# Down products paired across batch groups, products reordered and the down weights loaded later, in a fused attention and gated feed-forward kernel

## The chip, the cores and the metric

The kernel runs on one core of a Trainium2 chip. The metric is the time of one execution on the device, in microseconds (us); three runs of the kernel before gave 400.8, 400.87 and 401.26, and the median, 400.87, is its time.

The core has engines that work side by side, each through its own list of instructions in order: TensorE (PE: matrix products; PEld: the loading of their stationary operand), VectorE (DVE), ScalarE (ACT), GpSimd (POOL) and SyncE (SP). They wait for each other by semaphores. DMAs are issued from the lists of SP, ACT and POOL. A product's result lies in one of eight PSUM banks and must be read out by VectorE or ScalarE before the bank is used again.

## The reference

```python
# batch 8, 12 heads, 448 tokens, head_dim 64; d_model 768, d_ff 1536
scores = scale * np.matmul(q, k.transpose(0, 1, 3, 2)) - np.log(S)
attn = 1.0 / (1.0 + np.exp(-scores))
attn_out = np.matmul(attn, v)
x = attn_out.transpose(0, 2, 1, 3).reshape(B * S, H * D)      # 3584 x 768
gate = np.maximum(x @ w_gate, 0.0)
val = x @ w_val
out = gate * val @ w_out                                      # 3584 x 768, float32
```

## The kernel before

**Attention.** Batches 0 to 7 follow each other. A batch has three groups of four heads, and each group seven units of 64 keys: 21 qk units in all. A qk unit is four small products on quarters of the array into two banks, and two sigmoids on ScalarE into a PT tile. When a group's seven units are done, `pv_group` multiplies with v (28 small products, "pv"), and VectorE copies the two results into xT (`put_xT`, L184). The keys and queries are transposed by DMA from batch 2 on: VectorE copies them into `rel` (two copies for each group, L215) and SP issues the transpose into `qkT` (`dma_transposes`). `hold` is a copy of two elements on POOL that waits until such a transpose has landed, so that POOL's next load is issued behind it.

**Feed-forward.** Batches 0 and 1 form group 0, then 2 and 3 group 1, and so on. For group 0, gate and value are computed directly: `gv` makes one of 12 column blocks for one batch (two runs of six products of 448 columns) and VectorE writes relu(gate) * value into hT (L327). For groups 1 to 3 a "w" unit (`gv_pair`) does two column blocks for two batches with seven block products in place of eight (Strassen's scheme in Winograd's form). For the output, a "y" unit (`down_pair`) does two tiles of 128 tokens, tiles 2p and 2p+1, with seven products of six matmuls of 384 columns. With A the hT blocks (A11, A12 of the first tile, A21, A22 of the second; the second index is the half of d_ff) and B the four blocks of wo, the sums are S1 = A21+A22, S2 = S1-A11, S3 = A11-A21, S4 = A12-S2 and T1 = B12-B11, T2 = B22-T1, T3 = B22-B12, T4 = B21-T2, and the products are

P1 = A11 B11, P2 = A12 B21, P3 = S4 B22, P4 = A22 T4, P5 = S1 T1, P6 = S2 T2, P7 = S3 T3.

They are issued as P1 P5 P6 P2 P7 P3 P4, in y and in w units. P1, P6, P7 and P4 add up in one bank (u), P5 and P3 in a second, P2 has a third; in between, ScalarE and VectorE copy the partial sums out. Each group has 896 tokens, which is seven tiles: three y units and one odd tile, "t" (`down`), with twelve matmuls of 512 and twelve of 256 columns.

**Order.** In each batch the 21 qk units are dealt out over five or six stretches m (`cuts`). At the end of each stretch comes either a number of gv (`mix`, with `hooks` between them), or one unit of `work` by `next_work`; such a unit with its stretch is called a slot (a "y slot", a "w slot"). Stretches are counted from 0. `prepare` computes the sums (S) that the unit at the head of `work` needs; in a y unit it is called just before P4, so all four S of the following unit are made there by `token_sums`. `beside` runs the stretch's `jobs` (transposes, loads, sums of the next group's xT: `batch_sums_t1`, `batch_sums`). `gate_sums` turns wv's first half into wg-wv, which groups 1 to 3 need; `weight_sums` makes T1 to T4 of wo. Both are VectorE work.

In the kernel before, the order around the change is: wo is loaded in batch 1's last stretch, on POOL ahead of batch 3's k, q and v; T1 to T4 are made in batch 2's last two stretches; the first y unit (y0 of group 0) closes batch 2; the odd tile of group 0 stands in batch 3's stretch 3, followed by all six gate sums at once; y1 and y2 follow in batch 3's last stretch and batch 4's first. Group 1 starts in batch 4's stretch 1 and takes ten stretches (six w, t, y0, y1, y2), group 2 the next ten, and group 3 follows alone. The last pv stands between y1 and y2 of group 2.

Of the kernel before, what the change touches and what calls it, by code (L numbers as in the profile page):

```python
# [17 lines left out]
def kernel(  # L18
# [143 lines left out]
    def load_o():  # L162
        for m0, m1 in ((0, 512), (512, DM)):
            nc.gpsimd.dma_start(
                wo[:, :, m0:m1], moe_w_out[:, m0:m1].rearrange("(c p) m -> p c m", p=P)
            )
# [96 lines left out]
    class FirstSlot:  # L263
# [6 lines left out]
        def unit(self, u):  # L270
# [8 lines left out]
            i = (self.number * 4 + u) % 12  # L279
            PT = early.tile([P, 2, 512], FP16, tag=f"PT{i}", name="PT")  # L280
# [22 lines left out]

    def gv(b, q0, qn, f, act_relu):
# [19 lines left out]
        if g not in hT_tiles:  # L324
            hT_tiles[g] = hTp.tile([P, NFC, 2 * S], FP16, tag="hT", name="hT")
        o = (b % 2) * S + q0
        nc.vector.tensor_tensor(  # L327
            out=hT_tiles[g][:, f, o : o + qn],
            in0=gate_sb[:, 0:qn],
            in1=ps[1][:, 0:qn],  # L330
            op=AOP.mult,
        )
# [8 lines left out]
    def down(g, t):  # L341
        ysb = ysbp.tile([P, DM], FP32, tag="ysb", name="ysb")
        for nm, m0, m1 in (("ya", 0, 512), ("yb", 512, DM)):
            ps = bank(nm)
            for f in range(NFC):
                nc.tensor.matmul(  # L346
                    ps[:, 0 : m1 - m0],
                    hT_tiles[g][:, f, t * P : (t + 1) * P],
                    wo[:, f, m0:m1],
                    start=(f == 0),  # L350
                    stop=(f == NFC - 1),
                )
            nc.vector.tensor_scalar(
                out=ysb[:, m0:m1], in0=ps[:, 0 : m1 - m0], scalar1=OUT_SCALE, scalar2=None, op0=AOP.mult
            )
        store(g, t, ysb, 0, DM, (nc.sync, nc.sync))

# [7 lines left out]
    late = {}  # L365
    sums = {}

    def open_late():
        first_sbuf.close()
        pool = ctx.enter_context(tc.tile_pool(name="late", bufs=1))  # L370
        late["T"] = pool.tile([P, 4, HF, HM], FP16, tag="T", name="T")
        late["X"] = pool.tile([P, 3, HD, S], FP16, tag="X", name="X")
        late["sums"] = ctx.enter_context(tc.tile_pool(name="sums", bufs=2))
# [20 lines left out]

    def weight_sums(i):
        T = [late["T"][:, j] for j in range(4)]
        B11, B21 = wo[:, 0:HF, 0:HM], wo[:, HF:NFC, 0:HM]
        B12, B22 = wo[:, 0:HF, HM:DM], wo[:, HF:NFC, HM:DM]
        sub(T[i], *((B12, B11), (B22, T[0]), (B22, B12), (B21, T[1]))[i])

    def token_blocks(g, p):
        h = hT_tiles[g]
        t1, t2 = (slice(t * P, (t + 1) * P) for t in (2 * p, 2 * p + 1))
        return h[:, 0:HF, t1], h[:, HF:NFC, t1], h[:, 0:HF, t2], h[:, HF:NFC, t2]

    def token_sums(g, p):
# [3 lines left out]
        sub(S2, S1, A11)  # L410
        sub(S4, A12, S2)
        sub(A21, A11, A21)
        sums[("y", g, p)] = S1, S2, S4
# [9 lines left out]
    def down_pair(g, p, beside, then, last, first_copy):  # L423
        A11, A12, S3, A22 = token_blocks(g, p)
        S1, S2, S4 = sums.pop(("y", g, p))
        T1, T2, T3, T4 = (late["T"][:, i] for i in range(4))
        B11, B21, B22 = wo[:, 0:HF, 0:HM], wo[:, HF:NFC, 0:HM], wo[:, HF:NFC, HM:DM]
        y1, y2 = (ysbp.tile([P, DM], FP32, tag="ysb", name="ysb") for _ in range(2))
        lo, hi = slice(0, HM), slice(HM, DM)
        b, c, a = bank("u"), bank("y12"), bank("y11")  # L430
        later((7, 6, 5))
# [10 lines left out]
        first_copy(y1[:, lo], b)  # L442
        beside()
        product(c, S1, T1)
# [3 lines left out]
        product(a, A12, B21)  # L448
        plus(y1[:, lo], a)
        product(b, S3, T3, False)  # L450
        plus(y2[:, hi], b)
        product(c, S4, B22, False)
        plus(y1[:, hi], c)
        if last:
            store(g, 2 * p, y1, 0, DM, (nc.sync, nc.scalar))
        else:
            store(g, 2 * p, y1, 0, DM, (nc.sync, nc.sync))
# [3 lines left out]
        if last:  # L461
            store(g, 2 * p + 1, y2, HM, DM, (nc.sync, nc.sync))
            store(g, 2 * p + 1, y2, 0, HM, (nc.sync, nc.scalar))
        else:
            store(g, 2 * p + 1, y2, 0, DM, (nc.sync, nc.sync))
# [7 lines left out]
    def unit_sums(g, f):  # L473
        S1, S2, S4 = sums_tile(2 * P)
        fs = slice(f * P, (f + 2) * P)
# [5 lines left out]
        sums[("w", g, f)] = S1, S2, S4  # L481
# [10 lines left out]
    def batch_sums(g, ks):  # L492
        T1, T2, T4, _, B21, B12, B22 = batch_blocks(g, ks)
        sub(B12, B22, B12)
        sub(T2, B22, T1)
        sub(T4, B21, T2)

    def gv_pair(g, f, beside, first_copy):
# [3 lines left out]
        b, c, a = ([bank(nm) for _ in range(2)] for nm in ("u", "g2", "g1"))  # L502
        later((6, 7, 4, 5, 2, 3))
        gs = [[gsbp.tile([P, S], FP32, tag="gsb", name="gsb") for _ in range(3)] for _ in range(2)]
        if g not in hT_tiles:
            hT_tiles[g] = hTp.tile([P, NFC, 2 * S], FP16, tag="hT", name="hT")
        h = hT_tiles[g]
        sets = []
        for u in range(2):
            us, fs = slice(u * P, (u + 1) * P), slice((f + u) * P, (f + u + 1) * P)  # L510
            S1, S2, S4 = (t[:, :, us] for t in sums[("w", g, f)])
            sets.append((
                wg[:, 0:HD, fs], wg[:, HD:NDC, fs], wv[:, HD:NDC, fs],
                S1, S2, wv[:, 0:HD, fs], S4,
# [280 lines left out]
```

## Time and profile before

| what | us |
| --- | --- |
| median of three runs | 400.87 |
| the profiled execution, its own time | 400.93 |
| its span, first to last instruction | 399.2 |
| TensorE busy | 388.9 |
| VectorE busy | 279.9 |
| ScalarE busy | 223.0 |
| GpSimd busy | 49.4 |
| mean granted TensorE clock | 0.999 |

In a timeline each row is a run of equal instructions: start from the span's start, time from the first's start to the last's end, engine, line, operation, result<-inputs, shapes, count, and in brackets the idle time of the engine before it and what ended it. A row of TensorE ends later than the next one begins, as matmuls overlap; the time that a product takes of TensorE is therefore read from start to next start. Rows of "u", "y" and "g" on L385 are block products, "ya" and "yb" the odd tile, "g_ps" and "v_ps" a gv.

### The profile page before, as it was taken

Reading aid. Unit: us, or ns where it says so; the run is one execution under the profiler, and the core shown is the slowest. Engines: PE = TensorE matmul, PEld = TensorE weight load, DVE = VectorE, ACT = ScalarE, POOL = GpSimd, SP = SyncE. Lnnn points to the kernel's source line nnn. Section 1 sums busy time; section 2 is a strip of 40 time slices with the busy share of each in tenths; the row PEclk is TensorE's granted clock in tenths of the full one; section 3 lists DMA queues with packets and bytes.
Section 4 is the critical chain, followed back from the end, with each engine's and each line's share of the span. In section 5 each row is a group of like instructions: output and inputs, shape, how many; then the busy total and the mean of one; then the engine's idle time right before and its main releaser. Section 6 shows DMA issues by size and latency. Waiting matters only on the chain.

```text
span 399.2 us, 8737 instructions
## 1 busy us (share of the span) xinstructions
PE 388.9 (97%) x3488; PEld 217.9 (55%) x3488; DVE 279.9 (70%) x539; ACT 223.0 (56%) x475; POOL 49.4 (12%) x73
## 2 busy tenths in 40 slices
PE   8999999999998999999999999999999999999994
PEld 3678786545455554554555555455455555555562
DVE  2454344367358889999758889999766779887661
ACT  5946778783885565655665455565566234533131
POOL 8643301600030300003000300000000000000000
PEclk9999999999999999999999999999999999999999
DMA  9999994999897894224945695223012320000144
GB/s 149 199 199 204 205 141 94 177 203 187 178 161 152 165 204 76 46 48 51 178 85 133 130 218 89 48 24 61 12 40 80 80 79 2 0 2 0 39 115 124
DMA packets 68793, 43.69 MB, mean 109 GB/s; under 512 B 35856, under 2 KB 65296, under 8 KB 68752
## 3 DMA queue, kind: packets, MB, share of 16 engines
q0 software_dynamic: 30736, 23.33, 39.1%
q1 hardware_dynamic: 37584, 19.24, 23.0%
q8 instruction: 27, 0.44, 0.5%
q10 hardware_dynamic: 432, 0.56, 0.4%
q14 instruction: 14, 0.11, 0.1%
HBM read 47.19 MB, written 11.01 MB: 146 GB/s over the span
## 4 chain that ended last, share of the span: by engine, by line
PE 73%; DMA 14%; issue 6%; POOL 3%; DVE 2%; ACT 1%; ACTq 0%; POOLq 0%; DVEq 0%
PE u L385 32%; PE g L385 15%; PE y L385 9%; DMA v<-in_v_dram 6%; PE qk_ps L232 5%; PE pv_ps L250 5%; DMA wo<-in_moe_w_out_dram 4%; DMA k<-in_k_dram 4%; PE ya L346 3%; PE v_ps L309 1%; PE yb L346 1%; PE g_ps L309 1%; POOL q L110 1%; POOL k L110 1%; DVE wv L376 1%
## 5 line engine op out<-in xcount | busy, mean ns | idle before, releaser
L187 ACT ACTIVATE PT<-qk_ps 128x448 f16<-128x448 f32 (+3 forms) x318 | 150.6, 594 | 71.2 <-PE qk_ps L232 71.1
L385 PEld LDWEIGHTS <-S 128*128 128x128 f16 x540 | 52.8, 98 | 44.4 <-issue 0.8
L528 DVE TENSOR_TENSOR gsb<-g,gsb 128x448 f32<-128x448 f32 x72 | 43.0, 625 | 14.5 <-PE g L385 13.8
L232 PE MATMUL qk_ps<-qkT 64*64 64x448 f16 (+2 forms) x756 | 50.0, 336 | 0.9 <-DVE qkT L206 0.5
L421 ACT ACTIVATE ysb<-u 128x384 f32<-128x384 f32 x27 | 13.4, 498 | 56.3 <-PE u L385 56.3
L327 DVE TENSOR_TENSOR hT<-gate_sb,v_ps 128x256 f16<-128x256 f32 (+2 forms) x36 | 16.2, 465 | 33.5 <-ACT gate_sb L318 22.4
L385 PEld LDWEIGHTS <-hT 128*128 128x128 f16 x288 | 27.7, 98 | 21.0 <-issue 3.2
L524 ACT COPY gsb<-u 128x448 f32<-128x448 f32 x48 | 25.8, 566 | 23.9 <-PE u L385 22.9
L250 PE MATMUL pv_ps<-PT,v 64*64 64x448 f16 (+2 forms) x756 | 37.4, 329 | 0.4 <-issue 0.4
L184 DVE TENSOR_SCALAR xT<-pv_ps 128x448 f16<-128x448 f32 (+2 forms) x53 | 27.9, 567 | 13.4 <-PE pv_ps L250 12.1
L232 PEld LDWEIGHTS <-qkT 64*64 64x64 f16 x756 | 20.3, 105 | 24.9 <-issue 16.3
L309 PE MATMUL v_ps<-xT,wv 128*128 128x256 f16 (+2 forms) x216 | 33.3, 291 | 0.4 <-DVE hT L327 0.2
L309 PE MATMUL g_ps<-xT,wg 128*128 128x256 f16 (+2 forms) x216 | 33.5, 292 | 0.1
L385 PEld LDWEIGHTS <-wv 128*128 128x128 f16 x216 | 21.1, 98 | 19.8
L385 PEld LDWEIGHTS <-wg 128*128 128x128 f16 x216 | 20.3, 98 | 20.6 <-issue 3.0
L250 PEld LDWEIGHTS <-v 64*64 64x64 f16 x756 | 21.8, 107 | 11.8 <-issue 1.4
L385 PE MATMUL u<-T,hT 128*128 128x384 f16 x144 | 27.3, 326 | 0.0
L437 DVE SCALAR_TENSOR_TENSOR ysb<-y,ysb 128x384 f32<-128x384 f32 x24 | 13.4, 557 | 18.8 <-PE y L385 11.3
L110 POOL DMA_DIRECT2D k<-in_k_dram x14 | 10.9, 779 | 112.3 <-DVE rel L215 105.8
L309 PEld LDWEIGHTS <-wg 128*128 128x128 f16 x216 | 18.5, 98 | 11.5 <-issue 5.0
L309 PEld LDWEIGHTS <-wv 128*128 128x128 f16 x216 | 20.1, 98 | 8.2 <-DMA wv<-in_moe_w_val_dram 0.5
L385 PE MATMUL u<-xT,wg 128*128 128x448 f16 x108 | 23.5, 353 | 0.1
(67 smaller groups left out, 531.3 us busy)
## 6 DMA issues: line engine op xcount, KB each, us to landing
out_dram<-ysb SPq DMA_DIRECT2D x53, 192.0 KB, 2.9
k<-in_k_dram POOLq DMA_DIRECT2D x5, 672.0 KB, 11.8
q<-in_q_dram POOLq DMA_DIRECT2D x5, 672.0 KB, 14.9
v<-in_v_dram POOLq DMA_DIRECT2D x8, 336.0 KB, 15.6
v<-in_v_dram POOLq DMA_DIRECT2D x16, 168.0 KB, 15.3
k<-in_k_dram POOLq DMA_DIRECT2D x8, 224.0 KB, 10.4
wo<-in_moe_w_out_dram POOLq DMA_DIRECT2D x1, 1536.0 KB, 13.2
q<-in_q_dram POOLq DMA_DIRECT2D x6, 224.0 KB, 11.3
```

What stands on the lines that cost most here:

```text
L110: nc.gpsimd.dma_start(t16[:, xs, cs], rows_of(src, b)[:, xs, cs])
L184: nc.vector.tensor_scalar(out=xT, in0=src, scalar1=XSCALE, scalar2=None, op0=AOP.mult)
L187: nc.scalar.activation(PT_ap, ps_ap, AF.Sigmoid, bias=sig_bias, scale=qk_scale)
L232: nc.tensor.matmul(out_of(hh)[o : o + 64, :], qkT[rows, c, cols], qkT[rows, NCH + c0 : NCH + c1, cols], start=True, stop=True, tile_positi ...
L250: nc.tensor.matmul(ps[hh][64 * r : 64 * r + 64, 0:qn], v16[rows, 2 * g + hh, c * D : (c + 1) * D], pieces[c][rows, hh, :], start=(c == 0), ...
L309: nc.tensor.matmul(ps[-1][:, 0:qn], wt[:, dc, f * P : (f + 1) * P], xT_tiles[b][:, dc, q0 : q0 + qn], start=(dc == 0), stop=(dc == NDC - 1),)
L327: nc.vector.tensor_tensor(out=hT_tiles[g][:, f, o : o + qn], in0=gate_sb[:, 0:qn], in1=ps[1][:, 0:qn], op=AOP.mult,)
L346: nc.tensor.matmul(ps[:, 0 : m1 - m0], hT_tiles[g][:, f, t * P : (t + 1) * P], wo[:, f, m0:m1], start=(f == 0), stop=(f == NFC - 1),)
L385: nc.tensor.matmul(ps[:, 0:n], A[:, k_, :], W[:, k_, :], start=(first and k_ == 0), stop=(k_ == kn - 1), skip_group_check=True,)
L421: nc.scalar.activation(o, ps[:, 0:HM], AF.Copy, scale=OUT_SCALE)
L524: by(gs[u][i][:], ps[u][:, 0:S])
L528: nc.vector.tensor_tensor(out=gs[u][i][:], in0=ps[u][:, 0:S], in1=gs[u][i][:], op=AOP.add)
```

## The change

- The odd tiles are paired: for groups 0 and 2, tile 6 is written by the gating into a tile of its own, `aside`; the odd group that follows takes it as the first tile of a fourth y unit (p == 3), with its own tile 6 as the second. `down` is gone. Group 0 and 2 have three y units, groups 1 and 3 four.
- The gating is one function (`gated`) for gv and w units: max and product in one instruction, cut in two where a part goes to `aside` (batch 1's gv and group 2's odd half: 320 and 128 columns).
- Block products are issued as P1 P2 P5 P6 P3 P7 P4 in both kinds of unit. In a y unit S1 and S2 are still made a unit ahead; S4 and S3 (`more_token_sums`) now after P2, behind the stretch's jobs. y1's store follows P3.
- T3 is written over B12 inside wo; T has three parts.
- y0 of group 0 moves from the end of batch 2 to batch 3's stretch 3. The transposes of batch 3 move from y0's jobs into the hooks of batch 2's stretches 4 and 5. wo is loaded after them on POOL, behind a hold for group (3,1), in two DMAs of 768 full rows each, in place of two of all rows and 512 or 256 columns. T1 and T2 are made in batch 3's stretch 2, T3 and T4 in its stretch 3; the gate sums in batch 2's stretch 5, batch 3's stretch 0 and batch 4's stretch 2.
- A group's work is pushed with the last stretch of its second batch instead of after the next batch's first pv. The last w unit of a group gates in another order: in group 1 and 3 the odd batch first, then S1 and S2 of the next unit, then the even batch; in group 2 the even batch, then S1 and S2, and the odd batch in the next unit. The last pv and the last xT sums of batch 7 are jobs of its last stretch.
- In batch 0, the PT tiles of the first three slots have tags of their own size, and those of the other three come from the general ring `PTp`.

```diff
     def load_o():
-        for m0, m1 in ((0, 512), (512, DM)):
+        for i in range(2):
+            cs = slice(i * NFC // 2, (i + 1) * NFC // 2)
             nc.gpsimd.dma_start(
-                wo[:, :, m0:m1], moe_w_out[:, m0:m1].rearrange("(c p) m -> p c m", p=P)
+                wo[:, cs, :], moe_w_out.rearrange("(c p) m -> p c m", p=P)[:, cs, :]
             )
...
+            if self.number < NG:
+                PT = early.tile([P, 2, qn * len(cs)], FP16, tag=f"PT{self.number}{u}", name="PT")
+            else:
+                PT = PTp.tile([P, 2, S], FP16, tag="PT", name="PT")
...
+    ASIDE = 6 * P
+
+    def gated(g, f, o, n, gate_sb, val, relu=AOP.max):
...
+        end = o + n
+        cut = max(o, min(end, ASIDE)) if g % 2 == 0 else end
+        for a, z, dst in ((o, cut, hT_tiles[g]), (cut, end, late.get("aside"))):
+            if a < z:
+                d = 0 if dst is hT_tiles[g] else ASIDE
+                nc.vector.scalar_tensor_tensor(
+                    out=dst[:, f, a - d : z - d],
...
     def weight_sums(i):
-        T = [late["T"][:, j] for j in range(4)]
-        sub(T[i], *((B12, B11), (B22, T[0]), (B22, B12), (B21, T[1]))[i])
+        T1, T2, T4 = (late["T"][:, j] for j in range(3))
+        sub(*((T1, B12, B11), (T2, B22, T1), (B12, B22, B12), (T4, B21, T2))[i])
 
     def token_blocks(g, p):
...
+        if p == 3:
+            return late["aside"][:, 0:HF], late["aside"][:, HF:NFC], h[:, 0:HF, t1], h[:, HF:NFC, t1]
...
         nc.vector.tensor_tensor(out=S1, in0=A21, in1=A22, op=AOP.add)
         sub(S2, S1, A11)
+        sums["y"] = S1, S2, S4
+
+    def more_token_sums(g, p):
...
         sub(S4, A12, S2)
         sub(A21, A11, A21)
...
         product(b, A11, B11)
         first_copy(y1[:, lo], b)
+        product(a, A12, B21)
         beside()
+        plus(y1[:, lo], a)
         product(c, S1, T1)
         scaled_act(y2[:, hi], c)
         product(b, S2, T2, False)
         scaled_act(y1[:, hi], b)
-        product(a, A12, B21)
-        plus(y1[:, lo], a)
+        product(c, S4, B22, False)
+        plus(y1[:, hi], c)
+        store(*to1, y1, 0, DM, (nc.sync, nc.scalar if last else nc.sync))
         product(b, S3, T3, False)
         plus(y2[:, hi], b)
-        product(c, S4, B22, False)
-        plus(y1[:, hi], c)
...
+        if final == "even":
+            finish((True,))
+            prepare()
+            return lambda: finish((False,))
+        if final == "odd":
+            finish((False,))
+            prepare()
+            finish((True,))
+        else:
+            finish((True, False))
...
     def push_group(g):
-        tail = [("t", g, 6)] + [("y", g, p) for p in range(3)]
-        if g == 0:
-            tail.insert(0, tail.pop(1))
-        work.extend([("w", g, f) for f in range(0, NFC, 2) if g > 0] + tail)
+        if g > 0:
+            work.extend([("w", g, (f, f + 1)) for f in range(0, NFC, 2)])
+        work.extend([("y", g, p) for p in ((3, 0, 1, 2) if g % 2 else (0, 1, 2))])
...
+            down_pair(
+                g, i, lambda: (beside(), more_token_sums(g, i)), prepare, not work,
...
         elif b == 2:
-            mix = (2, 2, 1, 1, 1, 2)
+            mix = (2, 1, 2, 1, 2, 1)
             hooks = {
-                2: [(0, prepare)],
-                4: [(1, lambda: weight_sums(0)), (0, lambda: weight_sums(1))],
-                5: [(1, lambda: weight_sums(2)), (0, lambda: weight_sums(3))],
+                4: [(1, lambda: (dma_transposes(3, 0), dma_transposes(3, 1), hold(3, 1), load_o()))],
+                5: [(0, lambda: (dma_transposes(3, 2), gate_sums(0, 2), gate_sums(2, 4)))],
             }
...
         elif b == 3:
             mix = (1, 1, 1, 0, 0)
+            hooks = {
+                0: [(0, lambda: (gate_sums(4, 6), gate_sums(6, 8)))],
+                2: [(1, lambda: weight_sums(0)), (0, lambda: (weight_sums(1), prepare()))],
+            }
...
+            if b == 3 and m == count - 2:
+                jobs.append(lambda: (weight_sums(2), weight_sums(3)))
+            elif b == 4 and m == 2:
+                jobs.append(lambda: (gate_sums(8, 10), gate_sums(10, 12)))
...
                 if m == count - 1:
+                    push_group(b // 2)
                     jobs.append(lambda: (batch_sums_t1(b // 2), batch_sums(b // 2, (0, 1))))
+                    if b == B - 1:
+                        jobs.append(lambda: (pv_finish(b), batch_sums(b // 2, (1, HD))))
...
-            if b == 3 and m == 3:
-                for f in range(0, NFC, 2):
-                    gate_sums(f, f + 2)
-    pv_finish(B - 1)
-    push_group(B // 2 - 1)
-    next_work([lambda: batch_sums(B // 2 - 1, (1, HD))])
     while work:
         next_work((), True)
```

## The prediction

> **What bounds the kernel now.** I read the page's busy times first, then busy times in stretches of 10 us, then TensorE's own timeline, to see whether there is idle time to win or only work to remove.
>
> ```profile
> PE 388.9 (97%) x3488; PEld 217.9 (55%) x3488; DVE 279.9 (70%) x539; ACT 223.0 (56%) x475; POOL 49.4 (12%) x73
> ```
> ```profile
> 90.00:100.00 10.00, 9.35 (x54) 5.27 (x54) 7.87 (x13) 3.05 (x7) 0.00 (x0) 1.00 1.12 186
> ...
> 120.00:130.00 10.00, 8.85 (x78) 5.04 (x70) 8.91 (x21) 5.15 (x12) 0.00 (x0) 1.00 0.74 152
> ...
> 250.00:260.00 10.00, 10.00 (x76) 4.93 (x78) 9.80 (x19) 5.49 (x13) 0.00 (x0) 1.00 0.25 48
> ```
>
> The columns are PE, PEld, DVE, ACT, POOL, granted clock, DMA share, GB/s. TensorE is never idle after its start except near 95 and 122 us, at full clock; VectorE is at 8.9 to 9.8 of 10 in the group work. So the time is TensorE's list of products plus whatever makes it wait, and VectorE has little room. Timeline of TensorE:
>
> ```profile
> 96.17 1.14 PE L385 MATMUL u<-T,S 128*128 128x384 f16 x6 [0.57 <-DVE ysb L416]
> ...
> 115.21 2.77 PE L346 MATMUL ya<-wo,hT 128*128 128x512 f16 x12
> 117.81 1.47 PE L346 MATMUL yb<-wo,hT 128*128 128x256 f16 x12
> ...
> 123.14 1.14 PE L385 MATMUL u<-wo,hT 128*128 128x384 f16 x6 [1.16 <-DVE xT L184]
> 124.11 1.14 PE L385 MATMUL y<-T,S 128*128 128x384 f16 x6
> ```
>
> From start to next start, a product of a pair takes 0.975 us (123.14 to 124.11), an odd tile 4.0 us (115.21 to 119.22). Two waits can go: about 1.1 us around the weight sums (0.73 before 96.17, 0.36 in the stretch before it) and 1.3 us before 123.14, behind six gate sums.
>
> **What is removed.** (1) Pairing: four odd tiles of 4.00, 4.00, 4.00 and 3.90 us give 15.9; two pairs of 7 x 0.975 give 13.7. Gain 2.2. (2) y0 no longer runs in batch 2 and the gate sums are spread: gain 1.1 + 1.3 = 2.4. (3) The end: the last store on SP left at 395.72, after three others, while the last product ended near 393.7. With P3 and P7 ahead of P4 as now ordered, y1's store leaves one product (0.975) earlier; I take 0.9 (bounds 0 and 1.5). Together 5.5.
>
> **Down weights.** Before, both wo loads were issued at 70.9 and 71.95 and landed at 84.1 and 88.0. Now they stand on POOL behind a hold, a copy that waits for the transposed keys and queries of group (3,1). The rows of before that price this:
>
> ```profile
> 108.96 0.17 POOL L638 COPY gate<-qkT 1x2 f16<-1x2 f16 x1 [32.38 <-DMA qkT<-rel]
> 109.50 0.87 POOL L110 DMA_DIRECT2D k<-in_k_dram  x1 [0.36 <-issue]
> ```
> ```profile
> k<-in_k_dram POOLq DMA_DIRECT2D x1, 672.0 KB, 6.9
> ```
> ```profile
> wo<-in_moe_w_out_dram POOLq DMA_DIRECT2D x1, 1536.0 KB, 13.2
> wo<-in_moe_w_out_dram POOLq DMA_DIRECT2D x1, 768.0 KB, 16.1
> ```
>
> A k load after a hold, on quiet queues, landed 6.9 us after issue; in a row of loads 768 KB more took 3.94 us (84.11 to 88.05), some 195 KB per us. On the clock of before: the first gv of batch 2's stretch 4 ends at 87.8, as the counts up to it are equal (2+2+1+1 and 2+1+2+1). VectorE gates it in two pieces to 88.6; four copies to rel follow. In the profile the first transpose left 0.75 after its copy began (96.03, 96.78), the second 1.7 later, landing 4.4 after that: 89.35, 91.05, 95.45. The hold and the 0.54 after it put the first wo load at 96.05. It carries 1152 KB: 6.9 + 480/195 = 9.4, landing at 105.45; the second, 5.9 to 6.0 later, at 111.45. Batch 3's inputs, 2304 KB ahead of schedule, land some 12 us sooner, which nobody waited for. Behind the hold on POOL stand the second hold and batch 4's loads; these queue behind wo and land near 118 (k, q), before their copies near 125, so they cost nothing.
>
> The Trainium skill, "DMA: Bandwidth & Descriptors", section on the anatomy of one DMA on the SWDGE path, speaks against this price: a fixed 2.0 us plus bytes at 436 GB/s. By it the chunks (1.18 MB written, 2.36 MB read) would land 4.7 to 7.4 us after issue and 2.7 to 5.4 apart, and the sum would end 2.6 to 4 us lower. For the k load it gives 3.6 to 5.2 us where the row has 6.9, so the row decides.
>
> **y0, now in batch 3's stretch 3.** TensorE gets there so: gv to 90.25; qk and gv of stretch 5 (0.69 + 2.38) to 93.3; the first transposed tile lands at 93.45, so 0.3 of waiting; batch 3's stretches 0 to 2 (4.6, 3.55, 4.8) to 106.55; 16 qk to 107.7, held to 108.1 because the last gv's bank is freed by a gating that stands behind T1 = B12 - B11, which waits for 105.45. P1 ends 109.1. P2 reads rows of the second load: it starts at 111.55 and ends at 112.5. VectorE, in its own order: T2 (1.35, waiting for 111.45) to 112.95, S1 and S2 to 114.05, the copy of P1's bank to 114.5, T3 and T4 (1.35 each, 1.3 apart) to 117.1, S4 to 117.6, S3 to 118.1. So P5 starts at 113.5, P6 at 114.6, P3 at 117.65, and three products end at 120.6. Without any wait it is 114.5. Cost 6.1 + 0.3 = 6.4. If wo were there in time, VectorE's list alone (T2 to 108.85, S2 110, copy 110.5, T3, T4 113.1, S4 113.6) would make the slot end at 116.6: 2.1. That is the lower bound; the upper one is 8.1, with the second chunk landing 16.1 after its issue at 97.1, as the second wo row did.
>
> **S4 and S3 moved behind the jobs.** They were computed a slot ahead; now they follow the slot's other VectorE jobs, and P3, the fifth product, needs S4. The y1 slot of before shows the list:
>
> ```profile
> 124.31 0.56 DVE L416 TENSOR_SCALAR ysb<-u 128x384 f32<-128x384 f32 x1 [0.69 <-PE u L385]
> 124.79 0.38 DVE L215 COPY rel<-k 128x896 f16<-128x896 f16 x1
> ...
> 125.99 0.85 DVE L376 TENSOR_TENSOR X<-xT 128x1344 f16<-128x1344 f16 x1
> 126.88 0.39 DVE L376 TENSOR_TENSOR xT<-xT 128x448 f16<-128x448 f16 x1
> 127.19 0.81 DVE L376 TENSOR_TENSOR X<-xT,X 128x448 f16<-128x448 f16 x2
> 127.92 0.55 DVE L437 SCALAR_TENSOR_TENSOR ysb<-y,ysb 128x384 f32<-128x384 f32 x1
> ```
>
> S4 would take the place of the row at 127.92 and end at 128.5. P1 began at 123.14, so the fifth product wants 123.14 + 3.9 = 127.04: a wait of 1.45. The same reading of the other slots with batch sums: batch 4's stretch 0, S4 at 136.9 against 136.16, 0.8; batch 5's last, 219.5 against 218.67, 0.9; batch 6's first, 228.6 against 227.8, 0.8. Sum 3.95 (bounds 2 and 5). y slots without jobs end S4 a product early.
>
> **The last attention product inside a slot.** Batch 7's last y slot now holds pv of group 2 after P2. By the rows near 304: ten sigmoids end at 308.7, P2 at 308.4, so pv waits 0.4; on VectorE the T1 and first batch sums, xT and the last batch sums (1.81) end near 312.8, S4 at 313.4, wanted at 312.2: 1.2. Cost 1.6 (0.5 to 2.5).
>
> **w5 of group 1.** The odd half is gated before the even one, with S1 and S2 (1.1) between, and the even one frees the bank. In the profile gating began at 197.44; the even half would end at 200.8, and the third qk unit, whose turn is 199.6, needs that bank: 1.3 (0 to 2).
>
> **Small edits.** Two gate sums (1.0) in batch 4's stretch 2, a slot with no VectorE room: 0.8 (0 to 1.5). Split gatings: from 256 columns (422 ns) and 448 (621), 320 + 128 cost 780 ns, 0.16 more, 24 times; hidden by VectorE's slack of 9 us in batch 2 and 5.7 in group 2's 61 us; if that is gone, 1.9. P2 in second place gives the first copy two products of time; there was no wait there, so nothing gained. The other PT buffers, max folded into the gating (614 against 621 ns), sums' order: 0; one late sigmoid (0.6) is their bound.
>
> **Sum.** -5.5 + 6.4 + 3.95 + 1.6 + 1.3 + 0.8 = +8.55. Profiled execution 400.93 (span 399.2, 1.7 outside it), against a median of 400.87: **409.4 us**. All lower bounds together give 399.4, all upper ones 415.
>
> **Rivals.** (A) wo in time, as if chunk two landed by 106: y0 costs 2.1, time 405.4. For it: my landing rests on one load after a hold; against: every issue in the rows took 6.9 or more. (B) VectorE fills up: split gatings and gate sums push every w slot of groups 1 and 2 by 0.3, 12 x 0.3 = 3.6: 413. For it 9.8 of 10 at 250; against, its tail follows TensorE anyway. (C) Faster: S4 needs no waiting because VectorE, relieved of S4 and S3 at the slot's start, runs the jobs early, and wo is in time; then only 5.5 less y0's 2.1 counts, or all 5.5: 395.5 to 397.5. It decides from S4 ending 0.8 to 1.45 earlier in every y slot; against it, the copy of P1's bank starts the list, and that waits for P1. (D) The pairing doesn't save: 42 products of 384 columns against 12 of 512 and 12 of 256 twice; the durations above exclude that.
>
> **Chances.** Forecast 0.52, A 0.20, B 0.12, C 0.13, and 0.03 for a result near no change. Under 0.2% (0.8 us; the runs spread by 0.46) can't be told from none. The range leaves the corners out: A lies in it; below 402 lie C and the near-zero case, above 414 a small part of B. Slower 0.84, same 0.03, faster 0.13. The likeliest case alone: 406.5 to 412.
>
> **What would show it.** wo landing 9 and 15 us after issue near 96; T2 waiting for that DMA; TensorE idle before P2, P5 and P3 of y0; 0.8 to 1.5 of idle before the fifth product in the four slots with batch sums, ended by VectorE; a qk wait after group 1's w5. If wo lands before 106 and those gaps are absent, the prediction is wrong.

## The result, and the profile after

| | before | after |
| --- | --- | --- |
| median of four runs, us | 400.91 | 428.64 (428.23 to 430.05) |
| ratio to before, 95% interval | | 1.0696 [1.0671, 1.0722] |
| span of the profiled execution, us | 399.2 | 426.5 |
| mean granted TensorE clock | 0.999 | 0.996 |

The forecast was 409.4, range 402 to 414. The sign was right; the loss is 27.7 us where 8.5 were worked out. The page of the kernel after, busy times by engine:

```profile
PE 395.9 (93%) x3476; PEld 216.6 (51%) x3476; DVE 282.2 (66%) x570; ACT 229.8 (54%) x482; POOL 49.5 (12%) x74
```

TensorE, 97% busy before, is 93% busy in a span 27 us longer: it waits. Where, the list of waits of the kernel after says (engine, line, what was waited for; total us, times, longest us):

```profile
PE u L385 <- DVE ysb L445: 9.1, 14, 0.7
...
DVE T L376 <- DMA wo<-in_moe_w_out_dram: 5.9, 2, 4.2
...
PE y L385 <- DVE S L376: 4.5, 6, 1.2
...
PE u L385 <- DVE gsb L531: 3.6, 18, 0.5
...
PEld L251 <- DMA v<-in_v_dram: 2.2, 3, 0.8
```

The rows with the counts 14 and 18 are the new thing: there are 14 y units and 18 w units, and each has one such wait. TensorE's timeline of the kernel after, a y unit and, from another place, the end of a w unit:

```profile
210.92 1.15 PE L385 MATMUL u<-wo,aside 128*128 128x384 f16 x6
211.91 1.14 PE L385 MATMUL y<-wo,aside 128*128 128x384 f16 x6
212.88 1.14 PE L385 MATMUL y<-T,S 128*128 128x384 f16 x6
213.86 1.14 PE L385 MATMUL u<-T,S 128*128 128x384 f16 x6
214.84 1.14 PE L385 MATMUL y<-wo,S 128*128 128x384 f16 x6
215.81 1.14 PE L385 MATMUL u<-wo,hT 128*128 128x384 f16 x6
217.60 1.14 PE L385 MATMUL u<-T,hT 128*128 128x384 f16 x6 [0.65 <-DVE ysb L445]
```
```profile
164.44 1.30 PE L385 MATMUL u<-xT,wv 128*128 128x448 f16 x6
165.92 0.35 PE L385 MATMUL u<-X,wv 128*128 128x448 f16 x1 [0.18 <-DVE gsb L531]
```

The first seven rows are P1 P2 P5 P6 P3 P7 P4, one line each. The result names the bank: u, y, y, u, y, u, u. P7 and P4 are neighbours, and both add into u. Between them stands `plus(y2[:, hi], b)`, which must read P1 + P6 + P7 out of u before P4 adds to it. VectorE's timeline there (kernel after) shows that readout:

```profile
216.99 0.56 DVE L445 SCALAR_TENSOR_TENSOR ysb<-u,ysb 128x384 f32<-128x384 f32 x1 [0.35 <-PE u L385]
```

It can begin only when P7 is out of the pipeline (215.81 + 1.14 = 216.95) and lasts 0.56 us; P4 starts at 217.60. From the last matmul of P7 to P4's first is 0.975 us, where two matmuls otherwise follow at 0.163: 0.81 lost in each y unit, 11.36 us in 14. In w units the same step takes 0.533 where 0.190 is usual (0.85 in one of them); the 18 lose 6.49. **17.85 us in all.** Before, P3, in another bank, stood between P7 and P4, and TensorE worked while VectorE read. The kernel before has no gap there (TensorE's timeline, P7 P3 P4 of the y1 slot):

```profile
127.04 1.14 PE L385 MATMUL u<-T,hT 128*128 128x384 f16 x6
128.01 1.14 PE L385 MATMUL y<-wo,S 128*128 128x384 f16 x6
128.99 1.14 PE L385 MATMUL u<-T,hT 128*128 128x384 f16 x6
```

The y0 slot, where the forecast had its largest term, in TensorE's timeline and VectorE's (kernel after):

```profile
108.68 0.94 PE L233 MATMUL qk_ps<-qkT 64*64 64x448 f16 x13
110.81 0.38 PE L233 MATMUL qk_ps<-qkT 64*64 64x448 f16 x3 [1.19 <-DVE aside L320]
111.12 1.15 PE L385 MATMUL u<-wo,hT 128*128 128x384 f16 x6
114.91 1.61 PE L385 MATMUL y<-wo,hT 128*128 128x384 f16 x6 [2.65 <-DMA wo<-in_moe_w_out_dram]
116.84 2.10 PE L385 MATMUL y<-T,S 128*128 128x384 f16 x6 [0.32 <-DVE S L412]
118.74 1.21 PE L385 MATMUL u<-T,S 128*128 128x384 f16 x6
120.91 1.15 PE L385 MATMUL y<-wo,S 128*128 128x384 f16 x6 [0.96 <-DVE S L376]
```
```profile
108.80 1.36 DVE L376 TENSOR_TENSOR T<-wo 128x2304 f16<-128x2304 f16 x1 [1.73 <-DMA wo<-in_moe_w_out_dram]
...
114.96 1.36 DVE L376 TENSOR_TENSOR T<-wo,T 128x2304 f16<-128x2304 f16 x1 [4.21 <-DMA wo<-in_moe_w_out_dram]
...
120.30 0.55 DVE L376 TENSOR_TENSOR S<-hT,S 128x768 f16<-128x768 f16 x1
```

Each wait is the one foreseen: T1 for the first load, qk for the gating behind T1, P2 and T2 for the second load, P5 for S1, P3 for S4. From the slot's first qk (108.68) to P7 (121.89) it takes 13.2; without waits 1.23 + 5 x 0.975 = 6.1. So 7.1 are lost. P5 took 2.10 us in it, at half the clock, but that lengthened nothing: P3 still waited for S4 (the row at 120.30), and VectorE's list had run without a pause from T2 at 114.96 to there. Busy times in stretches of 1 us (columns as in the prediction, the granted clock third from the end):

```profile
115.00:116.00 1.00, 1.00 (x6) 0.46 (x6) 1.00 (x1) 0.00 (x0) 0.00 (x0) 0.73 1.26 205
116.00:117.00 1.00, 0.68 (x3) 0.13 (x2) 0.97 (x3) 0.00 (x0) 0.00 (x0) 0.50 1.26 203
117.00:118.00 1.00, 1.00 (x4) 0.45 (x3) 1.00 (x3) 0.00 (x0) 0.00 (x0) 0.50 1.28 207
118.00:119.00 1.00, 1.00 (x5) 0.48 (x4) 1.00 (x1) 0.02 (x1) 0.00 (x0) 0.56 1.26 206
```

One wait nobody had priced stands earlier, in batch 2 (TensorE's timeline of the kernel after):

```profile
74.23 0.38 PE L251 MATMUL pv_ps<-PT,v 64*64 64x448 f16 x2 [0.22 <-DMA v<-in_v_dram]
75.14 0.37 PE L251 MATMUL pv_ps<-PT,v 64*64 64x448 f16 x1 [0.53 <-DMA v<-in_v_dram]
75.98 1.51 PE L251 MATMUL pv_ps<-PT,v 64*64 64x448 f16 x25 [0.47 <-DMA v<-in_v_dram]
```

The mix gives stretch 1 one gv in place of two, so the pv of group (2,0) comes 2.3 us sooner, and v(2) landed only between 74.2 and 75.9. About 2.0 us.

### The profile page after: what moved, and what is told of

Same layout as the page of the kernel before. It is cut to its first block, busy times and chain, and to the rows that moved or that the text cites. A ratio compares the mean times of both kernels' runs of the same rounds, so it can differ in the third digit from the quotient of the medians.

```text
span 426.5 us, 8694 instructions
## 1 busy us (share of the span) xinstructions
PE 395.9 (93%) x3476; PEld 216.6 (51%) x3476; DVE 282.2 (66%) x570; ACT 229.8 (54%) x482; POOL 49.5 (12%) x74
## 4 chain that ended last, share of the span: by engine, by line
PE 58%; DVE 16%; DMA 15%; issue 7%; POOL 3%; ACT 1%; DVEq 0%; POOLq 0%; SPq 0%
PE u L385 27%; PE g L385 11%; DVE gsb L531 7%; PE y L385 7%; DMA v<-in_v_dram 7%; PE pv_ps L251 5%; PE qk_ps L233 5%; DMA wo<-in_moe_w_out_dram 4%; DMA k<-in_k_dram 3%; DVE ysb L445 2%; DVE X L376 1%; PE g_ps L334 1%; PE v_ps L334 1%; DVE S L376 1%; DMA qkT<-rel 1%
## 5 line engine op out<-in xcount | busy, mean ns | idle before, releaser
L385 PEld LDWEIGHTS <-S 128*128 128x128 f16 x576 | 56.0, 98 | 53.7 <-DVE S L376 6.8
L428 ACT ACTIVATE ysb<-u 128x384 f32<-128x384 f32 x32 | 15.7, 490 | 63.0 <-PE u L385 63.0
L385 PEld LDWEIGHTS <-hT 128*128 128x128 f16 x312 | 29.8, 98 | 35.8 <-issue 14.7
L320 DVE SCALAR_TENSOR_TENSOR hT<-gate_sb,v_ps 128x256 f16<-128x256 f32 (+2 forms) x36 | 14.6, 420 | 36.8 <-ACT gate_sb L343 23.1
L385 PEld LDWEIGHTS <-wv 128*128 128x128 f16 x216 | 21.0, 97 | 26.3 <-issue 8.2
L385 PE MATMUL u<-wo,hT 128*128 128x384 f16 x156 | 29.7, 327 | 0.1
L445 DVE SCALAR_TENSOR_TENSOR ysb<-y,ysb 128x384 f32<-128x384 f32 x28 | 15.5, 555 | 20.4 <-PE y L385 17.1
L527 ACT COPY gsb<-g 128x448 f32<-128x448 f32 x36 | 19.2, 533 | 14.2 <-PE g L385 13.3
L385 PE MATMUL u<-X,wv 128*128 128x448 f16 x108 | 23.3, 351 | 3.6 <-DVE gsb L531 3.6
## 6 DMA issues: line engine op xcount, KB each, us to landing
k<-in_k_dram POOLq DMA_DIRECT2D x8, 224.0 KB, 10.4
```

The costliest lines, as they stand in the source:

```text
L320: nc.vector.scalar_tensor_tensor(out=dst[:, f, a - d : z - d], in0=gate_sb[:, a - o : z - o], scalar=0.0, in1=val[:, a - o : z - o], op0=relu,
L385: nc.tensor.matmul(ps[:, 0:n], A[:, k_, :], W[:, k_, :], start=(first and k_ == 0), stop=(k_ == kn - 1), skip_group_check=True,)
L428: nc.scalar.activation(o, ps[:, 0:HM], AF.Copy, scale=OUT_SCALE)
L445: nc.vector.scalar_tensor_tensor(out=o, in0=ps[:, 0:HM], scalar=OUT_SCALE, in1=o, op0=AOP.mult, op1=AOP.add)
L527: by(gs[u][i][:], ps[u][:, 0:S])
```

## The experiments

Ratios are to the kernel before, run beside each on the same chip. "Gap" is the start-to-start excess over a matmul's usual distance.

### Only the order of products: b_new_order

The kernel before, with the change's order of products in y and w units and nothing else.

```diff
 product(b, A11, B11)
 first_copy(y1[:, lo], b)
+product(a, A12, B21)
 beside()
+plus(y1[:, lo], a)
 product(c, S1, T1)
 scaled_act(y2[:, hi], c)
 product(b, S2, T2, False)
 scaled_act(y1[:, hi], b)
-product(a, A12, B21)
-plus(y1[:, lo], a)
+product(c, S4, B22, False)
+plus(y1[:, hi], c)
 product(b, S3, T3, False)
 plus(y2[:, hi], b)
-product(c, S4, B22, False)
-plus(y1[:, hi], c)
```

> The kernel before with one part of the change alone: the products of its y and w units in the order P1 P2 P5 P6 P3 P7 P4, everything else as it was. Theory (bank read out between P7 and P4): 12 y units x 0.81 + 18 w units x 0.34 = 15.9, about 417 (414.5 to 418.5). Rival (the waits need the changed sums, gates and loads): within 3 us of 400.9.

Measured: 414.85 us, ratio 1.0348 [1.0328, 1.0368]. Its timeline shows the wait where there was none in the rows of before from 127.04 on:

```profile
127.19 1.14 PE L385 MATMUL y<-wo,S 128*128 128x384 f16 x6
128.16 1.14 PE L385 MATMUL u<-T,hT 128*128 128x384 f16 x6
129.95 1.14 PE L385 MATMUL u<-T,hT 128*128 128x384 f16 x6 [0.65 <-DVE ysb L437]
```

The gaps before P4 sum to 9.73 in 12 y units and 6.18 in 18 w units, 15.9. Against that, the time from the last product's last matmul to the end of the span falls from 5.64 to 4.36 (y1 is done a product earlier), and a wait of 0.73 near 96 is gone, where P6 of y0 waited for the first copy of P1's bank (the prediction's row at 96.17): 15.9 - 1.28 - 0.73 = 13.9, and the spans of the two profiled executions, 413.1 and 399.2, differ by 13.9. So the order of products alone makes the kernel slower by 3.5%.

### The order of before in the kernel after: a_old_order

The kernel after with the diff above reversed, in y and w units; everything else of the change kept.

> The changed kernel with one part undone: the block products of the y and w units again in the order P1 P5 P6 P2 P7 P3 P4; loads, sums, pairing and slots stay as changed. Theory (P7 and P4 add to one bank, and between them that bank must be read out; with P3 between them the readout is covered): the waits of 0.81 us before the last product of 14 y units and of 0.34 before that of 18 w units go, 11.4 + 6.2 = 17.6 us, to about 411 (409 to 413; S3 is then needed a product earlier, up to 0.5 in each of four slots). Rival (VectorE is simply late in these units, whatever the order): the waits move to another product and the time stays above 422.

Measured: 416.94, ratio 1.0408 [1.0369, 1.0446]. The gaps before P4 are gone, so the rival falls, but the time is some 5 us above the theory's. The timeline (of an execution of 419.72) shows what was overlooked:

```profile
113.95 1.15 PE L385 MATMUL u<-wo,hT 128*128 128x384 f16 x6
119.92 2.10 PE L385 MATMUL y<-T,S 128*128 128x384 f16 x6 [4.82 <-DVE S L412]
121.81 2.12 PE L385 MATMUL u<-T,S 128*128 128x384 f16 x6
123.73 2.12 PE L385 MATMUL y<-wo,hT 128*128 128x384 f16 x6
```

With P5 second, S1, which stands behind T2 on VectorE and so behind the second half of wo, is wanted a product sooner, and the three products after the wait run at half the clock. The end of the span takes 5.69 us again where the kernel after has 4.37. So this run mixes several terms, and later ones take wo's wait away first.

### The sums S4 and S3 ahead: a_sums_ahead

```diff
-    def prepare():
+    def prepare(more=True):
...
                 token_sums(g, i)
+                if more:
+                    more_token_sums(g, i)
```

`prepare(False)` stays in the last w units, and a flag keeps the sums from being made twice.

> The changed kernel with one part altered: S4 and S3 of a y unit are again made a unit ahead, with S1 and S2 (only the first y unit behind a w unit keeps them in its own slot). Theory (P3 waits for S4 behind the slot's other VectorE work): the waits of 1.4, 0.6, 0.8, 0.6 and 1.1 us before the fifth product of five slots go, and some 1 us in y0's slot: about 424 (422.5 to 425.5). Rival (they move to the readout before P4): no change, 428 to 429.

Measured: 422.87, ratio 1.054 [1.0521, 1.0558]. 5.8 us below the kernel after, whose six gaps before P3 sum to 5.5. The gaps before P4 stay (0.81 in each y unit).

### The down weights earlier: a_early_wo and a_split_wo

a_early_wo issues v(2) and both halves of wo before the hold for (2,1), and drops the hold for (3,1).

> The changed kernel with one part altered: batch 2's v and then the down weights are issued on GpSimd right behind batch 2's keys and queries, ahead of the hold for (2,1), and the hold for (3,1) is gone; products in the changed order. Theory (y0's slot waits for the second wo load, and batch 2's second pv waits for v): some 6 us of y0's 7.2 and the 2.0 before the pv go, about 421 (419 to 423); the clock stays at full speed around y0. Rival (VectorE's list in y0's slot is the cause, and the load only looks like it): at least 425.

Measured: 433.47, ratio 1.0806 [1.0779, 1.0833]: slower than the kernel after, against the expectation. The y0 slot has no wait for wo any more, but TensorE's timeline shows a larger one elsewhere:

```profile
62.28 0.66 PE L334 MATMUL v_ps<-xT,wv 128*128 128x192 f16 x6
73.87 0.96 PE L233 MATMUL qk_ps<-qkT 64*64 64x448 f16 x8 [10.94 <-DMA qkT<-rel]
```

The DMA transpose of (2,0) was issued at 55.13, after the loads (52.82 and 53.69), and landed at 73.83, 0.5 behind the second half of wo (73.36): 18.7 us, where the same transpose took 5.4 in the kernel after (55.73 to 61.09) and one on free queues 4.1 (91.62 to 95.72). So holding the loads back does real work.

a_split_wo keeps the hold and issues only the first half early:

```diff
         hold(2, 1)
         load_v(2)
+        load_o(0)
...
-            mix = (2, 1, 2, 1, 2, 1)
+            mix = (2, 2, 1, 1, 2, 1)
...
-dma_transposes(3, 1), hold(3, 1), load_o()
+dma_transposes(3, 1), hold(3, 1), load_o(1)
```

> The changed kernel with its loads altered and nothing else of its products or sums: the first half of the down weights is issued right behind batch 2's v (as before, ahead of batch 3's inputs), the second half stays behind the hold for (3,1); and batch 2's stretches take 2 2 1 1 2 1 gv in place of 2 1 2 1 2 1, so that its second pv comes when v has landed. Theory (y0 waits for the second half, pv for v, and the clock drop follows from these waits): the second half lands 9 to 10 us after its issue instead of 15 to 16, the 2 us before the pv and some 5 of the 7 in y0's slot go: about 421.5 (419 to 423.5). Rival (y0's slot is bound by VectorE's list, loads matter little): above 426.

Measured: 421.25, ratio 1.0498 [1.0485, 1.0512], as the theory had it. The halves land at 81.73 and 107.81, the second 11.3 us after its issue where 9 to 10 were expected, and the waits inside y0 are down to the one for S4, ahead of the readout before P4:

```profile
109.60 1.14 PE L384 MATMUL y<-wo,hT 128*128 128x384 f16 x6
110.57 1.14 PE L384 MATMUL y<-T,S 128*128 128x384 f16 x6
111.55 1.14 PE L384 MATMUL u<-T,S 128*128 128x384 f16 x6
114.11 1.15 PE L384 MATMUL y<-wo,S 128*128 128x384 f16 x6 [1.42 <-DVE S L375]
```

### The mix alone: a_mix

The kernel after with batch 2's mix 2 2 1 1 2 1, and nothing else.

> The kernel after with batch 2's mix 2 2 1 1 2 1 in place of 2 1 2 1 2 1 and nothing else; the hold and the wo loads keep their place behind seven gv. My theory (the early pv of group (2,0) waits 2.0 us for v(2), and everything behind it, the hold and wo's issue included, comes that much later): the wait goes, the y0 slot keeps its length because TensorE and the load of wo both come 2 us earlier: 428.64 - 2.0 = 426.6, 425.8 to 427.4. Rival (the load of wo lands at a time that the DMA queues set, not the hold, so that the 2 us come back as a longer wait before P2): 428 or more.

Measured: 425.81, ratio 1.0612 [1.0594, 1.0629]; 2.8 below the kernel after, at the lower edge of the theory's range. The pv runs without a wait, wo is issued 2.3 sooner (96.11) and lands 2.3 and 2.7 sooner (106.43, 112.18). The early pv was worth 2.0 to 2.8.

### The order of products once more: a_split_old and a_swap

a_split_old is a_split_wo with the order of before.

> The kernel after with the product order of before (as in a_old_order) and, as in a_split_wo, the first half of wo issued right behind v(2), the second behind the hold, and batch 2's mix 2 2 1 1 2 1. This separates the order of products from the waits for wo, v and S1 that fell on each other in a_old_order. My theory (the readout between P7 and P4 costs 0.81 us in a y unit and about 0.35 in a w unit, 17.6 in all): the 421.25 of a_split_wo falls by 17.6, and S3, which P7 now needs a product earlier, gives back about 0.5 in each of five job slots: 406, 404 to 408. TensorE's idle time before P4 is 0 in all y and w units. Rival (the order of before is worth only the 11.7 that a_old_order showed, because part of the 17.6 is taken again by other waits that come with that order everywhere): 409.5 or more, with waits spread over all units.

Measured: 408.17, ratio 1.0183 [1.0167, 1.0198]: 0.2 above the theory's range and below the rival's. There is no gap before P4 in any unit. The gaps before P7, where S3 is waited for, sum to 8.0 where those before P3 summed to 5.9: 2.1 for the 2.5 that the theory gave. What it left out is the end of the span, 5.62 against 4.36, and two gaps behind P1 (0.44 and 0.50), where P5 in second place finds S1 not ready: 406 + 1.27 + 0.94 = 408.2.

a_swap makes the smallest edit: in the kernel after, P7 and P3 change places.

```diff
-        product(c, S4, B22, False)
-        plus(y1[:, hi], c)
-        store(*to1, y1, 0, DM, (nc.sync, nc.scalar if last else nc.sync))
         product(b, S3, T3, False)
         plus(y2[:, hi], b)
+        product(c, S4, B22, False)
+        plus(y1[:, hi], c)
+        store(*to1, y1, 0, DM, (nc.sync, nc.scalar if last else nc.sync))
```

> The kernel after with one edit: P7 and P3 change places in y and w units (P1 P2 P5 P6 P7 P3 P4), so that P7 and P4, which add into one bank with a readout between them, are no longer neighbours; P2 stays in second place. My theory (the neighbourhood alone is the 17.9 us of gaps before P4): those gaps fall to 0; S3, which the fifth product now needs, is made one VectorE sum (0.45) after S4, so six job slots wait 0.45 longer, 2.7; the stores of the end lose the 1.27 that the order of a_split_wo had over that of a_split_old. 428.64 - 17.9 + 2.7 + 1.3 = 414.8, 413 to 416.5. Rival (the cost comes from P2 in second place, which takes the third bank early, and not from the neighbours): no change, 425 or more, and the gaps before P4 stay or turn up before another product.

Measured: 424.83, ratio 1.0592 [1.0575, 1.061]: 10 us above the theory and next to the rival's 425. The gaps left P4 and turned up before P7, 0.74 or more in each y unit and 0.22 in each w unit. With P2 in second place P6 and P7 become neighbours, both in u, with the copy of u to y1 on ScalarE between them, which the theory overlooked. So P2's place matters, though not for the third bank that the rival named. The last run of the next part shows this with most of the other waits gone.

### All repairs together: a_joined, a_joined_even, a_swap_joined

a_joined keeps the pairing, the slots and the spread gate sums; it takes the order of products of before, S4 and S3 ahead, a_split_wo's load and mix, and T1 a stretch earlier.

> Everything that the runs point to, with the pairing, the slots and the gate sums of the change kept: products in the old order, S4 and S3 a unit ahead (in y0 ahead of T3 and T4), the split load with 2 2 1 1 2 1, and T1 made a stretch earlier. Theory (the terms add up): 428.6 - 17.9 (readout between P7 and P4) - 2.0 (v) - 6.5 (y0) - 4.4 (S4) = 397.8 (396.5 to 400.5), so a little faster than the kernel before. Rival (the pairing and the shift cost something of their own that these terms cover): 403 or more.

Measured: 401.01, ratio 0.9994 [0.9984, 1.0003]: no difference that can be told, and 0.5 above the expected range. Its timeline shows a wait that is left behind group 1's last w unit:

```profile
193.39 1.49 PE L250 MATMUL pv_ps<-PT,v 64*64 64x448 f16 x28
195.50 0.35 PE L232 MATMUL qk_ps<-qkT 64*64 64x448 f16 x1 [0.61 <-DVE hT L319]
```

The odd batch is gated first there, and the even one's gating frees the bank. a_joined_even removes that:

```diff
-        work.extend([("y", g, p) for p in ((3, 0, 1, 2) if g % 2 else (0, 1, 2))])
+        work.extend([("y", g, p) for p in ((0, 1, 2, 3) if g % 2 else (0, 1, 2))])
...
-                rest = gv_units(g, i, beside, first_copy, ("even", "odd")[g % 2])
+                rest = gv_units(g, i, beside, first_copy, "even")
```

> a_joined with the last w unit of every group gating the even batch first and the odd batch in the next unit, and the y units of odd groups in the order 0 1 2 3, so that the unit of the odd tiles comes last. In a_joined TensorE still waited 1.1 us for a pv and a qk bank at 194.5 (behind group 1's last w unit) and 0.5 at 365.8 (behind group 3's). My theory (these are the odd-first gating and the y unit that needs the odd tile first): both waits go, 401.0 becomes 399.5 (398.8 to 400.3), which is faster than the kernel before by about 0.4%. Rival (the gating only moves, and the next unit's list on VectorE is late by the same amount): 400.7 to 401.5, with waits of 1 us or more in the y unit that follows.

Measured: 399.69, ratio 0.9971 [0.9961, 0.9981], as expected in time. Of the two waits that it names only the first is gone: before P5 of group 3's first y unit (366.61) 0.5 us are still lost, though that unit no longer holds the odd tiles. It waits there for S1, as in y0. TensorE's list of waits in this kernel:

```profile
PE qk_ps L232 <- DMA qkT<-rel: 1.2, 1, 1.2
...
PE y L384 <- DVE S L411: 0.6, 2, 0.3
```

This kernel is 29 us below the kernel after and has the lowest time of this study. a_swap_joined is the same with P2 in second place: P1 P2 P5 P6 P7 P3 P4.

> a_joined_even with P2 in second place: P1 P2 P5 P6 P7 P3 P4 in place of P1 P5 P6 P2 P7 P3 P4. It keeps every other part of the change (pairing, y0 in batch 3, the early P2, the spread gate sums). My theory (P2's place costs nothing as long as P7 and P4 are apart): 399.7 (399.0 to 400.6), no gap before P4. Rival (P2 in second place leaves P6 and P7 as neighbours on one bank with a readout between them, as P7 and P4 were, so that the gap moves there): some 0.8 for each y unit and 0.34 for each w unit again, 411 or more.

Measured: 412.97, ratio 1.0296 [1.028, 1.0311]: the rival, not the theory. TensorE's timeline and ScalarE's in this kernel:

```profile
309.47 1.14 PE L384 MATMUL u<-T,S 128*128 128x384 f16 x6
311.19 1.14 PE L384 MATMUL u<-wo,hT 128*128 128x384 f16 x6 [0.58 <-ACT ysb L431]
```
```profile
310.65 0.49 ACT L431 ACTIVATE ysb<-u 128x384 f32<-128x384 f32 x1 [0.48 <-PE u L384]
```

P6 leaves at 309.47 + 1.14 = 310.61, ScalarE reads u from 310.65 for 0.49, P7 starts at 311.19. The gaps: 0.74 in each of 14 y units and 0.22 in each of 18 w units, 14.35; the time rose by 13.3, as some 1.1 us of waiting behind P1 for S1 (0.5 in y0, 0.5 in group 3's first y unit) went with P2 in second place. So neither P2's place nor P7's is free: whichever product into u has no product into another bank behind it pays its readout. u gets four products with three readouts between them, and just three products go to other banks. The kernel before puts one into each place: P1 (P5) P6 (P2) P7 (P3) P4.

### The gate sums spread in the kernel before: b_spread

```diff
             mix = (1, 1, 1, 0, 0)
+            hooks = {
+                0: [(0, lambda: (gate_sums(0, 2), gate_sums(2, 4)))],
+                1: [(0, lambda: (gate_sums(4, 6), gate_sums(6, 8)))],
+            }
...
-                for f in range(0, NFC, 2):
+                for f in range(8, NFC, 2):
```

> The kernel before with one small part of the change: four of its six gate sums are made in batch 3's stretches 0 and 1 (two each, behind their gv), two stay in stretch 3. Theory (the six at once hold the xT copies and with them TensorE for 1.3 us near 122): about 399.7 (399.3 to 400.3). Rival (the wait has another cause, such as the sigmoids): no change within 0.4.

Measured: 400.0, ratio 0.9975 [0.9966, 0.9984], as expected: the wait of 1.16 us before 123.14 in the prediction's rows is gone (TensorE's timeline of this kernel; the row has no idle time in brackets):

```profile
122.04 1.15 PE L385 MATMUL u<-wo,hT 128*128 128x384 f16 x6
```

It is 0.25% faster than the kernel before with five lines of code, and its interval overlaps that of a_joined_even, which needs the whole change with its repairs.

## Why the prediction was wrong

Its sum, term by term; "measured" is from the trace of the kernel after, and from a run where one is named.

| term | predicted | measured |
| --- | --- | --- |
| order of products, readouts of u | 0 | +17.85 (b_new_order: 13.9 net) |
| wait of pv for v(2), from the mix | 0 | +2.0 (a_mix: 2.8) |
| y0 slot and the qk before batch 3 | +6.4 | +7.4 |
| S4 behind the jobs, four slots | +3.95 | +3.3 |
| last pv in the y slot | +1.6 | +1.1 |
| w5 of group 1 | +1.3 | +0.9 |
| two gate sums in batch 4 | +0.8 | 0 |
| pairing | -2.2 | -2.2 (length of the products; not run alone) |
| T and gate sums moved | -2.4 | -2.4 (b_spread alone: -1.2 for 1.3) |
| end of the span | -0.9 | -1.3 |
| sum | +8.55 | +26.65 of 27.3 |

**The step that failed** is the sentence "P2 in second place gives the first copy two products of time; there was no wait there, so nothing gained", with the "three products end at 120.6" before it. It put the reordering at 0; it cost 17.85 us. It priced it by the wait that it could remove and never asked which product was new beside which. (Even that wait was there: its own row at 96.17 shows P6 waiting for the first copy, ended by L416, and in b_new_order it is gone.) What was needed stood in the text: P1, P6, P7 and P4 share a bank, with readouts between. Written as banks, before is u y u y u y u, after is u y y u y u u. Most of the cost could be worked out from the prediction's own rows: 0.55 us for an ysb readout on L437, plus the 1.14 - 0.975 that a product still runs after its last matmul's turn, an estimate of 0.7 for each y unit where 0.81 was measured.

The Trainium skill has the rule that bears on this. "PSUM — Partial Sum Buffer", section "Summary: rules for kernel authors", says that who reads PSUM while a matmul runs should have that matmul in another bank. The rows above agree: a product that goes on adding into the bank that is read waits 0.65 us, and with P3 between there is no wait.

**The second omission** is the mix. The prediction used the counts up to stretch 4, which are equal, to place the hold, and did not look at what the shift inside them does to the pv in stretch 2; v(2)'s landing is in the trace of before, so the 2.0 could have been read.

**Right in mechanism, off in size.** wo was forecast 9.4 and 15.4 us after the first issue; it landed 10.4 and 16.5 after (98.41 to 108.77 and 114.87), and the issue came 2.4 late, most of it the wait for v. The y0 slot lost 7.1 where 6.1 was forecast: the second half of wo landed 6.2 us after the slot's first qk (108.68 to 114.87) where 4.9 were forecast (106.55 to 111.45), and from there VectorE's list led to P3 in 6.0 us (114.87 to 120.91) where 6.2 were forecast. The four S4 waits were 1.37, 0.57, 0.76 and 0.57 for 1.45, 0.8, 0.9 and 0.8, each ended by VectorE as told. The two gate sums in batch 4 found room. The pairing's 2.2 was not run by itself. Some 0.7 us of the difference I can't place.

The rule that was weighed for wo, 2.0 us plus bytes at 436 GB/s from the Trainium skill ("DMA: Bandwidth & Descriptors", the section on the anatomy of one DMA on the SWDGE path), gives an estimate of at most 7.4 us after each issue; the trace has 10.4 and 15.6.

Three smaller readings were off without deciding anything. The 0.3 of waiting before batch 3 is 0.15 by its own times (93.3 and 93.45); the trace has 0.26. VectorE at 8.9 to 9.8 of 10 holds for most stretches of w units; from 200 to 230 us, in the y units, the kernel before has 5.7 to 8.2. And not every issue took 6.9 us or more: the three loads of v(2) took 5.6 to 5.8.

**The rivals.** B, that VectorE fills up, does not show: it is 66% busy, and nearly all that the w units newly wait for is the readout. The 0.34 there is close to B's 0.3 by chance: it is gone in all 18 with the order of before (a_old_order). A and C both needed wo in time; a_split_wo gave it that, and 7.4 came back, 2.8 of it by the mix alone. With most waits repaired (a_joined_even) the whole change gains 1.3 us of the 5.5 that were summed as removed, and b_spread gains 1.2 with the gate sums alone. So no gain of the pairing and the later y0 can be told from none; in a_joined_even 1.2 us of waiting for a transposed tile and 1.0 us of gaps inside y0 stand against it.

## What to carry to other kernels

When products that accumulate are put in another order, write down the bank of each, mark the readouts, and look for two neighbours on one bank with a readout between: each such pair costs the readout plus the pipeline's tail (0.81 us for 384 columns on VectorE, 0.74 on ScalarE), in every unit. And a count that comes out equal at the end of a stretch says nothing of what was moved forward inside it: follow every load that the moved work reads.

## What the hardware showed that I had not expected

- **The clock falls after different lengths of idle TensorE.** In the y0 slot TensorE was idle for 2.65 us, with 1.19 us of idle a product earlier, and the granted clock went to 0.50 some 0.5 us into the next product; by the stretches of 1 us it stayed so for 0.54 + 1 + 1 + 0.88 = 3.4 us, with matmuls at 320 ns where 163 is usual. In a_early_wo it fell 3.4 us into an idle time of 10.94, in a_old_order 3.8 us into one of 4.82 and was low for 6.8 (0.95 in 110 to 120, 0.71 in 120 to 130). In a_mix it fell only 0.5 us into one of 2.30, with 1.38 us of idle a product earlier, and was low for 6.8. The gaps of 1.0 to 1.8 us in the slots with jobs of a_split_old left it at 1.00. The Trainium skill, "TensorE: Matmul & The Clock Gate", Part 1, gives half rate after an idle window of about 3.4 us, and full rate after about 3.4 us of work. The drop in a_early_wo and the low stretch of 3.4 us agree; in the y0 slot and in a_mix less idle time was enough, and two low stretches were twice as long.
- **A DMA transpose can come out behind loads that were issued before it.** In a_early_wo, with 2304 KB of wo ahead from another engine's list, it took 18.7 us in place of 5.4, and the next one, issued at 63.66, landed 2.0 us behind wo as well.
- **In a w unit the same neighbourhood costs less**: 0.34 on VectorE and 0.22 on ScalarE, for 448 columns, by the code because each product is made for two column blocks in turn, so that the readout of the first block's bank runs beside the second block's product. No run took the blocks apart.
